# Attention beside two large products: the softmax bias on another engine, value products further behind, and rings of other lengths

## The chip, the cores and the metric

The kernel runs on one core of one Trainium2 chip. The metric is device time in microseconds (us) of one execution. A profiled execution is recorded by the hardware profiler; its span runs from the first instruction to the last. The engines are TensorE (PE; PEld is its weight load), VectorE (DVE), ScalarE (ACT), GpSimd (POOL) and SyncE (SP), which issues nearly all the DMAs. Each engine works through its own queue in order.

## The reference

Two branches are computed from two inputs and set side by side in the output. The first is attention over 2048 positions with 32 heads of 32, where a query sees itself and the 255 keys before it, followed by a product with `wo`. The second is a Fourier mixing layer, as products with given matrices.

```python
qkv = (x @ wqkv).reshape(B, S, 3, H, Dh)           # S 2048, H 32, Dh 32
scores = einsum("bhqd,bhkd->bhqk", q, k) * Dh ** -0.5
mask = (idx[:, None] - idx[None, :] >= 0) & (idx[:, None] - idx[None, :] < 256)
p = softmax(where(mask, scores, -1e9)); o = p @ v
a = o.reshape(B, S, D) @ wo

re = einsum("bsd,ed->bse", xb, dft_hid_re); im = einsum("bsd,ed->bse", xb, dft_hid_im)
b = einsum("ts,bse->bte", dft_seq_re, re) - einsum("ts,bse->bte", dft_seq_im, im)
out = concatenate([a, b], axis=-1)
```

## The kernel before

All products run in 16-bit halves: a value is split into a high half (ACT) and a low half (DVE subtracts the high half from the value), and a product is three passes over the halves. The large products are also taken as seven products of sums and differences of blocks instead of eight, so DVE, POOL and ACT make many sums, splits and evictions beside TensorE.

The program has three parts in time. First come the query, key and value projections. From the middle of these to nearly the end of the Fourier products, attention runs as a side stream between the large products. At the end stands the product with `wo`.

Attention works on 256 blocks. A block is two heads (`hp` picks a pair of the four in a group `g`) times 128 queries (`i`), within a chunk of 512 positions (`sc`). The first 128 blocks take the chunks 0 and 1 of all eight groups, the second 128 the chunks 2 and 3. For one block, `s_step` does this:

- scores on PE (L586) into `s`, and into `old` the oldest 128 keys, which need only a triangle; DVE merges the two (L597) and takes the negative row maxima (`mx`, L602);
- `bias` = maximum times scale plus a shift, on two columns (L609 on POOL; the code holds the same step for ACT at L606, chosen by the constant `BIAS`);
- two exponentials on ACT with that bias (L612), the split into `hl` (ACT L432, DVE L436), a transpose by DMA from SP into `t` (L621), and two mask selects on POOL: `z` from `t` (L627), then `t` in place (L630).

`v_step` takes two blocks: value products on PE into the one bank `pv` (L662), then on DVE a reciprocal, a sum and a multiply into the output `o` (L667 to L673). It stands `LAG` blocks behind the scores. `o_step`, once per group and chunk, splits `o` (ACT L432, DVE L436), transposes it (L684) and stores it (L687). A new group and chunk loads its keys, queries and values with DMAs (`qk1`, `qk0`, `vt`, all through L417); from chunk 2 on the second half of the chunk before is loaded again ahead of the chunk's own keys.

Every buffer belongs to a ring of fixed length. The first instruction that writes buffer k of a ring of n waits for all that use buffer k - n.

What sets the order is a planner inside the program. Every operation is entered with its engine, a cost and what it reads and writes. A due time is worked back from the places of TensorE's work: PE's operations in the order entered, the rest so early that PE is not late. A list scheduler with these costs then picks on each engine the ready operation that is due first. The result is written out as a fixed order for each engine, so a changed constant or ring length changes the order everywhere. `tick` advances attention by one block each time that a set share of the large product's matmuls has been entered.

The large products' own helpers, which the profile names: operands `st` and `reg` from `raw` (ACT L1101, DVE L1102), sums on POOL (L1075), evictions on ACT and DVE (L1193, L1509, L1512).

Of the kernel before, what the change touches and what calls it, by code (L numbers as in the profile page):

```python
# [10 lines left out]
F32 = mybir.dt.float32  # L11
F32R = mybir.dt.float32r
F16 = mybir.dt.float16
# [4 lines left out]
ALU = mybir.AluOpType  # L18
AX = mybir.AxisListType

P = 128
# [3 lines left out]
DH = 32  # L25
HG = 4
# [3 lines left out]
CH = 512  # L30
# [11 lines left out]
DOWN = 2.0 ** -25  # L42
UP = 2.0 ** 25

LAG = 4
LAST = 5
STP = 4
RAWS = 6
TBUF = 6
BIAS = "POOL"  # L50
SUMS = ("POOL", "POOL", "POOL", "POOL")
XSUM = "DVE"
PLAIN = 3
# [280 lines left out]
def fused_kernel(ctx: ExitStack, tc: tile.TileContext, xa, wqk, wv, wo, xb, wd, cs, out):  # L334
# [178 lines left out]
    def att_ring(tag, shape, dtype, n):  # L513
        r = Ring(R, lambda k: pool["att"].tile(shape, dtype, tag=tag, bufs=n, name=f"{tag}_{k}"), n)
        att_rings[tag] = r
        return r

    k_ring = att_ring("qk1", [96, HG, CH], F16, 3)
    q_ring = att_ring("qk0", [96, HG, CH], F16, 2)
    vt_ring = att_ring("vt", [P, QB, HG * VW], F16, 3)  # L520
    mx_ring = att_ring("mx", [P, 2], F32, 6)
    bias_ring = att_ring("bias", [P, 2], F32, 6)
    hl_ring = att_ring("hl", [P, 8 * P], F16, 3)
    t_ring = att_ring("t", [P, 8, P], F16, TBUF)
    z_ring = att_ring("z", [P, 4, P], F16, 4)
    rs_ring = att_ring("rs", [P, 2, 2], F32, 2)
    o_ring = att_ring("o", [P, QB * P], F32, 3)

    def attention():
        blocks = [(g, 2 * pr + sc, hp, i) for pr in range(2) for g in range(NG) for sc in range(2)  # L530
# [103 lines left out]
        def v_step(b):  # L634
            g, sc, hp, i = blocks[b]
            pv = pv_ring.new()
            pvt = lambda: pv.t[:, :4 * VW].rearrange("p (r h w) -> p r h w", r=2, h=2)
            if (g, sc) not in cur:
                cur[g, sc] = o_ring.new()
            for r in (1, 0):  # L640
                qb = sc * QB + i + r
                nb = min(qb + 1, 3)
                nt = min(nb, 2)
                d = st[b + r]
                mats, keys, cost = [], [(d["t"], 0), (d["t"], 1)] + ([d["z"]] if "z" in d else []), 0.0
                seq = [(0, kb) for kb in range(nb)] + [(1, kb) for kb in range(nb)]
                for j in range(2):
                    at = (2 * hp + j) * VW
                    for m, (part, kb) in enumerate(seq):
                        lo = DH * part  # L650
                        k = qb + 1 - nb + kb
                        keys.append(vts[g, k // QB])
                        mats.append((j, lo, part, kb, k, at, m == 0, m == len(seq) - 1, vts[g, k // QB]))
                        cost += 0.0265 if part else 0.0297

                def run(mats=mats, d=d, nb=nb, nt=nt, r=r):
                    for j, lo, part, kb, k, at, a, e, vt in mats:
                        if nb == 3 and kb == 0:
                            lhs = d["z"].t[:, part * 2 + j]
                        else:  # L660
                            lhs = d["t"].t[:, (part * 2 + j) * nt + kb - (nb - nt)]
                        nc.tensor.matmul(pvt()[:, r, j, lo:], lhs, vt.t[:, k % QB, at + lo:at + VW],  # L662
                                         start=a, stop=e, skip_group_check=True)

                op("PE", cost, run, r=list(dict.fromkeys(keys)), w=[pv])
            o, rs = cur[g, sc], rs_ring.new()
            dve(0.173, lambda: nc.vector.reciprocal(rs.t, pvt()[:, :, :, 2 * DH]), r=[pv], w=[rs])  # L667
# [5 lines left out]
            dve(0.29, lambda: nc.vector.tensor_tensor(  # L673
                o.t.rearrange("p (i c) -> p i c", i=QB)[:, i:i + 2, hp * 64:hp * 64 + 64]
                .rearrange("p r (h d) -> p r h d", d=DH), os_(),
                rs.t.unsqueeze(3).to_broadcast([P, 2, 2, DH]), op=ALU.mult), r=[pv, rs], w=[(o, hp, i)])

        def o_step(g, sc):
            o = cur.pop((g, sc))
            keys = [(o, hp, i) for hp in range(2) for i in (0, 2)]  # L680
            ohl, ot = o_ring.new(), o_ring.new()
            half = lambda h: (lambda: ohl.t.bitcast(F16).rearrange("p (h c) -> p h c", h=2)[:, h])
            split(half(0), half(1), lambda: o.t, None, 512, keys, [(ohl, 0)], [(ohl, 1)])
            op("SP", C_TURN, lambda: nc.sync.dma_start_transpose(  # L684
                ot.t.bitcast(F16).rearrange("p (a q) -> p a q", q=P), ohl.t.bitcast(F16)),
               r=[(ohl, 0), (ohl, 1)], w=[ot], dma=turned(8))
            op("SP", C_ISSUE, lambda: nc.sync.dma_start(ots[sc, :, g].rearrange("c h t -> c (h t)"), ot.t.bitcast(F16)),  # L687
               r=[ot], w=[dkey("o", sc, g)], dma=wire(256))

        for b in range(nblk + LAG):  # L690
# [1004 lines left out]
```

## Time and profile before

| | us |
|---|---|
| median of three runs | 1726.13 |
| the three runs | 1724.79, 1728.37, 1726.13 |
| profiled execution, own time | 1728.84 |
| its span | 1727.1 |
| PE busy in the span | 1690.3 |
| DVE, ACT, POOL busy | 1358.8, 1051.5, 771.6 |
| mean granted clock of TensorE | 0.998 of full |

The first scores start at 262 us and the last value products end at 1509 us. Matmuls overlap in the pipeline, so a group's mean duration (379 ns for a matmul of 512 columns) is longer than the distance between two starts. An engine's idle time is named with what ended it, and a wait for several semaphores is put down to the one that came last.

### The profile page before, as it was taken

Reading aid. Unit: us, or ns where it says so; the run is one execution under the profiler, and the core shown is the slowest. Engines: PE = TensorE matmul, PEld = TensorE weight load, DVE = VectorE, ACT = ScalarE, POOL = GpSimd, SP = SyncE. Lnnn points to the kernel's source line nnn. Section 1 sums busy time; section 2 is a strip of 40 time slices with the busy share of each in tenths; the row PEclk is TensorE's granted clock in tenths of the full one; section 3 lists DMA queues with packets and bytes.
Section 4 is the critical chain, followed back from the end, with each engine's and each line's share of the span. In section 5 each row is a group of like instructions: output and inputs, shape, how many; then the busy total and the mean of one; then the engine's idle time right before and its main releaser. Section 6 shows DMA issues by size and latency. Waiting matters only on the chain.

```text
span 1727.1 us, 31901 instructions
## 1 busy us (share of the span) xinstructions
PE 1690.3 (98%) x11607; PEld 908.6 (53%) x11607; DVE 1358.8 (79%) x2294; ACT 1051.5 (61%) x1678; POOL 771.6 (45%) x979
## 2 busy tenths in 40 slices
PE   8999999999999999999999999999999999999998
PEld 3446687675555445555544555545555545544443
DVE  6978997677988888777897986899985679879641
ACT  7555635456757788776675665776665576543322
POOL 0133501224535565635755755676664667611000
PEclk9999999999999999999999999999999999999999
DMA  6388799999998789998599998779999669983331
GB/s 266 121 329 326 229 309 272 267 244 244 221 278 204 159 200 246 215 273 194 98 233 274 246 278 175 151 153 255 238 261 224 141 129 207 215 264 110 110 98 74
DMA packets 469918, 368.36 MB, mean 213 GB/s; under 512 B 341760, under 2 KB 412416, under 8 KB 469760
## 3 DMA queue, kind: packets, MB, share of 16 engines
q1 hardware_dynamic: 468896, 363.17, 81.6%
q0 software_dynamic: 864, 3.15, 1.2%
q8 instruction: 91, 1.49, 0.4%
q14 instruction: 67, 0.55, 0.1%
HBM read 195.97 MB, written 96.86 MB: 170 GB/s over the span
## 4 chain that ended last, share of the span: by engine, by line
PE 83%; DVE 6%; ACT 4%; DMA 3%; issue 3%; POOL 1%; SPq 0%; POOLq 0%; DVEq 0%; ACTq 0%
PE m L720 74%; PE pv L662 4%; PE s L586 3%; PE old L586 1%; DVE st L1102 1%; DMA raw<-in_cs_dram 1%; DVE reg L439 1%; ACT junk L1001 1%; PE m L1323 1%; ACT s L612 1%; ACT reg L432 0%; DVE top L457 0%; DVE mx L602 0%; DVE s L597 0%; DMA late<-in_wo_dram 0%
## 5 line engine op out<-in xcount | busy, mean ns | idle before, releaser
L720 PE MATMUL m<-reg,st 128*128 128x512 f16 x4776 | 1101.1, 379 | 17.5 <-DVE st L1102 3.8
L720 PEld LDWEIGHTS <-st 128*128 128x128 f16 x5400 | 512.4, 98 | 579.1 <-issue 22.0
L612 ACT ACTIVATE s<-s,bias,escs 128x256 f32<-128x256 f32 (+1 forms) x512 | 270.5, 529 | 225.3 <-POOL bias L609 216.3
L609 POOL TENSOR_SCALAR bias<-mx,escs 128x2 f32<-128x2 f32 x256 | 114.2, 446 | 392.2 <-DVE mx L602 334.8
L1075 POOL TENSOR_TENSOR raw<-raw,raw 128x512 f32<-128x512 f32 x128 | 177.4, 1386 | 202.2 <-DVE st L1102 179.8
L436 DVE TENSOR_TENSOR hl<-s,hl 128x512 f16<-128x512 f32 (+1 forms) x256 | 170.6, 668 | 67.6 <-ACT hl L432 64.9
L627 POOL TENSOR_SCALAR_AFFINE_SELECT z<-t 128x512 f16<-128x512 f16 x224 | 174.2, 782 | 53.8 <-DMA t<-hl 41.3
L602 DVE TENSOR_REDUCE mx<-s 128x2 f32<-128x512 f32 (+1 forms) x256 | 170.8, 668 | 4.9
L630 POOL TENSOR_SCALAR_AFFINE_SELECT t<-t 128x512 f16<-128x512 f16 x224 | 169.5, 765 | 9.9
L432 ACT ACTIVATE hl<-s 128x512 f16<-128x512 f32 (+1 forms) x256 | 147.8, 578 | 8.2 <-DMA t<-hl 5.0
L720 PEld LDWEIGHTS <-reg 128*128 128x128 f16 x1212 | 116.3, 98 | 67.2 <-issue 5.2
L1101 ACT ACTIVATE st<-raw,sc 128x1024 f16<-128x1024 f32 x96 | 109.6, 1145 | 59.4 <-PE m L720 30.0
L1102 DVE SCALAR_TENSOR_TENSOR st<-raw,sc,st 128x1024 f16<-128x1024 f32 x96 | 135.8, 1418 | 11.9 <-ACT st L1101 10.7
L586 PEld LDWEIGHTS <-qk 96*128 96x128 f16 x1056 | 93.9, 98 | 81.5 <-issue 8.3
L597 DVE COPY_PREDICATED s<-upper,old 128x256 f32<-128x256 uint32 x224 | 94.6, 422 | 46.6 <-PE old L586 27.2
L720 PE MATMUL m<-reg 128*128 128x512 f16 x480 | 116.3, 382 | 3.5 <-ACT ybig L1509 3.0
L1512 DVE SCALAR_TENSOR_TENSOR ybig<-m,fu,ybig 128x512 f32<-128x512 f32 x112 | 83.4, 745 | 25.4 <-PE m L720 20.9
L720 PE MATMUL m<-xz,st 128*128 128x512 f16 x432 | 97.3, 379 | 2.7 <-ACT m L1193 2.5
L662 PE MATMUL pv<-vt,t 128*128 128x65 f16 x1984 | 98.3, 185 | 0.2
L586 PE MATMUL s<-qk,qk 96*128 96x128 f16 (+1 forms) x608 | 96.1, 253 | 2.0 <-DVE hl L436 1.5
L662 PEld LDWEIGHTS <-t 128*128 128x128 f16 x1984 | 88.3, 96 | 10.8 <-POOL t L630 0.4
L1001 ACT ACTIVATE junk<-raw 128x1024 uint8<-128x1024 f32 x82 | 86.3, 1052 | 10.2 <-DMA raw<-in_cs_dram 9.9
(172 smaller groups left out, 2130.9 us busy)
## 6 DMA issues: line engine op xcount, KB each, us to landing
raw<-in_cs_dram SPq DMA_DIRECT2D x64, 512.0 KB, 5.7
qk<-qs SPq DMA_DIRECT2D x192, 128.0 KB, 3.8
out_dram<-ybig SPq DMA_DIRECT2D x44, 512.0 KB, 4.9
qs<-ybig SPq DMA_DIRECT2D x64, 256.0 KB, 4.5
raw<-in_xb_dram SPq DMA_DIRECT2D x32, 512.0 KB, 5.3
raw<-in_wd_dram SPq DMA_DIRECT2D x32, 512.0 KB, 5.9
ybig<-out_dram SPq DMA_DIRECT2D x32, 512.0 KB, 4.9
vs<-ybig SPq DMA_DIRECT2D x32, 260.0 KB, 4.7
```

The costliest lines, as they stand in the source:

```text
L432: else nc.scalar.activation(dst(), src(), AF.Copy), r=r, w=w)
L436: op("DVE", c_dve(n), lambda: nc.vector.tensor_tensor(dst(), src(), hi(), op=ALU.subtract), r=r, w=w, port=port)
L586: nc.tensor.matmul(dst(j, a, e), qu.t[:, h, i * P:i * P + P], ku.t[:, h, ka:ke], start=True, stop=True, skip_group_check=True)
L602: dve(c_dve(2 * w), lambda: nc.vector.tensor_reduce(mx.t, sv(), axis=AX.X, op=ALU.max, negate=True), r=[(S, 0), (S, 1)], w=[mx])
L609: op("POOL", 0.28, lambda: nc.gpsimd.tensor_scalar(bias.t, mx.t, es, PSHIFT, op0=ALU.mult, op1=ALU.add), r=[mx, ("esc", g // 2)], w=[bias] ...
L612: op("ACT", 0.32 + 0.00085 * w, lambda h=h: nc.scalar.activation(sv()[:, h], sv()[:, h], AF.Exp, bias=bias.t[:, h:h + 1], scale=es), r=[bi ...
L627: op("POOL", 0.637, lambda: nc.gpsimd.affine_select(out=z.t, in_=pk(), compare_op=ALU.is_gt, fill=0.0, base=0, pattern=[[0, 4], [-1, P]], ...
L630: op("POOL", 0.637, lambda: nc.gpsimd.affine_select(out=pk(), in_=pk(), compare_op=ALU.is_ge, fill=0.0, base=0, pattern=[[0, 4], [1, P]], ...
L662: nc.tensor.matmul(pvt()[:, r, j, lo:], lhs, vt.t[:, k % QB, at + lo:at + VW], start=a, stop=e, skip_group_check=True)
L720: nc.tensor.matmul(ps.t[:, j * n:j * n + n], lhs(), rhs(), start=first, stop=last, skip_group_check=True)
L1075: lambda: e.tensor_tensor(o(), a(), b(), op=ALU.subtract if sub else ALU.add), r=r, w=w, port=True)
L1102: op("DVE", c_dve(n, True), lambda: nc.vector.scalar_tensor_tensor(dst(1), src(), scl(), dst(0), op0=ALU.mult, op1=ALU.subtract), r=[*r, s ...
```

## The change

- `BIAS` is "ACT": the bias of a block is an activation on ACT (L606) in place of an instruction on POOL (L609).
- `LAG` 4 becomes 6: value products stand six blocks behind the scores. The rate of `tick` follows from `LAG`, by two blocks in 262.
- `TBUF` 6 becomes 8: eight transposed tiles `t`.
- Keys `qk1` 3 to 2 buffers, values `vt` 3 to 2, masked tiles `z` 4 to 3, outputs `o` 3 to 1.
- `o_step` writes the output's halves into a buffer of the `hl` ring and transposes them into one of the `t` ring, where it took two of the `o` ring. Together they give what the two more `t` tiles take.
- The first value product of a group and chunk reads a key "turn", which the last multiply into the output before it writes.

```diff
-LAG = 4
+LAG = 6
-TBUF = 6
-BIAS = "POOL"
+TBUF = 8
+BIAS = "ACT"
...
-    k_ring = att_ring("qk1", [96, HG, CH], F16, 3)
+    k_ring = att_ring("qk1", [96, HG, CH], F16, 2)
-    vt_ring = att_ring("vt", [P, QB, HG * VW], F16, 3)
+    vt_ring = att_ring("vt", [P, QB, HG * VW], F16, 2)
-    z_ring = att_ring("z", [P, 4, P], F16, 4)
+    z_ring = att_ring("z", [P, 4, P], F16, 3)
-    o_ring = att_ring("o", [P, QB * P], F32, 3)
+    o_ring = att_ring("o", [P, QB * P], F32, 1)
...
-            if (g, sc) not in cur:
+            begins = (g, sc) not in cur
+            if begins:
                 cur[g, sc] = o_ring.new()
...
-                op("PE", cost, run, r=list(dict.fromkeys(keys)), w=[pv])
+                op("PE", cost, run, r=list(dict.fromkeys(keys)) + (["turn"] if begins else []), w=[pv])
...
-                rs.t.unsqueeze(3).to_broadcast([P, 2, 2, DH]), op=ALU.mult), r=[pv, rs], w=[(o, hp, i)])
+                rs.t.unsqueeze(3).to_broadcast([P, 2, 2, DH]), op=ALU.mult), r=[pv, rs], w=[(o, hp, i)] + (["turn"] if hp == 1 and i == 2 else []))
...
-            ohl, ot = o_ring.new(), o_ring.new()
-            half = lambda h: (lambda: ohl.t.bitcast(F16).rearrange("p (h c) -> p h c", h=2)[:, h])
+            ohl, ot = hl_ring.new(), t_ring.new()
+            half = lambda h: (lambda: ohl.t.rearrange("p (h c) -> p h c", h=2)[:, h])
...
```

How the order moves, at three places. A name's first number is its place in its ring's sequence: `s_136` holds the scores of block 136.

On ACT, blocks 136 and 137. Before:

```order
L612 ACTIVATE s_136_11519<-s_136_11519,bias_136_11542,escs_109 128x256 x2
L432 ACTIVATE hl_136_11568<-s_136_11519 128x512
L612 ACTIVATE s_137_11462<-s_137_11462,bias_137_11557,escs_109 128x256 x2
L1101 ACTIVATE st_97_11587<-raw_139_11046,sc_14_11555 128x1024
L1101 ACTIVATE reg1_81<-raw_138_11029,sc_14_11555 128x512
L432 ACTIVATE hl_137_11649<-s_137_11462 128x512
```

Now:

```order
L606 ACTIVATE bias_136_11418<-mx_136_11407,pshift_88,escs_109 128x2
L612 ACTIVATE s_136_11342<-s_136_11342,bias_136_11418,escs_109 128x256 x2
L431 ACTIVATE reg2_82<-raw_149_11316,vwd_103 128x1024
L606 ACTIVATE bias_137_11445<-mx_137_11432,pshift_88,escs_109 128x2
L612 ACTIVATE s_137_11389<-s_137_11389,bias_137_11445,escs_109 128x256 x2
L432 ACTIVATE hl_153_11472<-s_137_11389 128x512
```

The bias stands on ACT just ahead of its exponentials and waits there for DVE's maxima; an operand of the large products stands between the two blocks.

On POOL, sums for the operands and the mask selects around blocks 136 to 140. Before:

```order
L609 TENSOR_SCALAR bias_138_11665<-mx_138_11640,escs_109 128x2
L1075 TENSOR_TENSOR raw_138_11029<-raw_138_11029 128x512
L1075 TENSOR_TENSOR raw_138_11029<-raw_138_11029,raw_139_11046 128x512
L609 TENSOR_SCALAR bias_139_11721<-mx_139_11700,escs_109 128x2
L1075 TENSOR_TENSOR raw_139_11046<-raw_139_11046,raw_138_11029 128x512
L627 AFFINE_SELECT z_104_11740<-t_136_11585 128x512
L609 TENSOR_SCALAR bias_140_11761<-mx_140_11749,escs_109 128x2
L630 AFFINE_SELECT t_136_11585<-t_136_11585 128x4x128
```

Now:

```order
L1076 TENSOR_TENSOR raw_142_11414<-raw_142_11414,raw_141_11448 128x512
L1076 TENSOR_TENSOR raw_141_11448<-raw_141_11448 128x512
L627 AFFINE_SELECT z_108_11918<-t_156_11777 128x512
L627 AFFINE_SELECT z_107_11924<-t_155_11810 128x512
L630 AFFINE_SELECT t_156_11777<-t_156_11777 128x4x128
L630 AFFINE_SELECT t_155_11810<-t_155_11810 128x4x128
```

No bias stands between sums and selects any more.

On SP, around the second load of keys for group 1 of the second half (`qk1_20`), which the scores of block 144 need. Before, `t_138` to `t_141` are the blocks' own transposes:

```order
L621 DMA_TRANSPOSE t_138_11725<-hl_138_11709 128x8x128
L417 DMA qk1_20_11743<-qs_57 32x4x512 x3
L417 DMA raw_144_11755<-in_cs_dram 128x1024
L417 DMA ybig_83<-out_0_dram 128x1024
L417 DMA raw_145_11776<-in_cs_dram 128x1024
L621 DMA_TRANSPOSE t_139_11793<-hl_139_11757 128x8x128
L621 DMA_TRANSPOSE t_140_11825<-hl_140_11790 128x8x128
```

Now, where the output's halves count in the rings too (`t_157` is block 141's, `t_159` block 142's, `t_158` an output's):

```order
L621 DMA_TRANSPOSE t_157_11858<-hl_157_11842 128x8x128
L417 DMA qk1_20_11872<-qs_57 32x4x512 x3
L417 DMA qk0_19_11920<-qs_57 32x4x512
L621 DMA_TRANSPOSE t_159_11933<-hl_159_11905 128x8x128
L685 DMA_TRANSPOSE t_158_11950<-hl_158_11922 128x8x128
L417 DMA qk0_19_11920<-qs_57 32x4x512 x2
```

The load stood ahead of the transposes of blocks 139 to 143; it now stands behind those of 139 to 141, and ahead of two more.

More of the change, by code (lines that the diff above doesn't have):

```diff
@@ L680, in o_step @@
             keys = [(o, hp, i) for hp in range(2) for i in (0, 2)]
-            ohl, ot = o_ring.new(), o_ring.new()
-            half = lambda h: (lambda: ohl.t.bitcast(F16).rearrange("p (h c) -> p h c", h=2)[:, h])
+            ohl, ot = hl_ring.new(), t_ring.new()
+            half = lambda h: (lambda: ohl.t.rearrange("p (h c) -> p h c", h=2)[:, h])
             split(half(0), half(1), lambda: o.t, None, 512, keys, [(ohl, 0)], [(ohl, 1)])
-            op("SP", C_TURN, lambda: nc.sync.dma_start_transpose(
-                ot.t.bitcast(F16).rearrange("p (a q) -> p a q", q=P), ohl.t.bitcast(F16)),
+            op("SP", C_TURN, lambda: nc.sync.dma_start_transpose(ot.t, ohl.t),
                r=[(ohl, 0), (ohl, 1)], w=[ot], dma=turned(8))
-            op("SP", C_ISSUE, lambda: nc.sync.dma_start(ots[sc, :, g].rearrange("c h t -> c (h t)"), ot.t.bitcast(F16)),
+            op("SP", C_ISSUE, lambda: nc.sync.dma_start(ots[sc, :, g].rearrange("c h t -> c (h t)"),
+                                                        ot.t.rearrange("p a q -> p (a q)")),
                r=[ot], w=[dkey("o", sc, g)], dma=wire(256))
```

## The prediction

> **What bounds the kernel now.** I read the page's totals and chain first, then busy time by stage, then who ends TensorE's waits. In the page's first part each engine has busy us, share and instructions; in its chain, shares of the span.
>
> ```profile
> span 1727.1 us, 31901 instructions
> PE 1690.3 (98%) x11607; PEld 908.6 (53%) x11607; DVE 1358.8 (79%) x2294; ACT 1051.5 (61%) x1678; POOL 771.6 (45%) x979
> PE 83%; DVE 6%; ACT 4%; DMA 3%; issue 3%; POOL 1%; SPq 0%; POOLq 0%; DVEq 0%; ACTq 0%
> ```
>
> TensorE sets the end; it is idle for 1727.1 - 1690.3 = 36.8 us. The change adds or removes no matmul, so it can only move this idle time. Where it lies, from a table of stretches (length, then busy us and instructions of PE, PEld, DVE, ACT, POOL; clock; DMA):
>
> ```profile
> 0.00:262.00 262.00, 253.09 (x1529) 152.62 (x1529) 221.80 (x284) 149.07 (x197) 62.46 (x69) 1.00 0.75 263
> 262.00:590.00 328.00, 327.94 (x2510) 193.59 (x2510) 257.86 (x457) 204.31 (x350) 134.81 (x202) 1.00 0.97 239
> 590.00:625.00 35.00, 30.39 (x213) 14.93 (x212) 31.59 (x69) 29.77 (x53) 15.31 (x18) 1.00 0.78 175
> 625.00:860.00 235.00, 234.91 (x1701) 122.44 (x1700) 184.51 (x348) 176.91 (x299) 136.62 (x171) 1.00 0.86 206
> 860.00:960.00 100.00, 94.59 (x649) 47.48 (x648) 87.54 (x158) 66.72 (x106) 59.85 (x68) 1.00 1.03 253
> 960.00:1130.00 170.00, 169.89 (x1320) 90.42 (x1319) 136.05 (x255) 112.05 (x192) 108.48 (x144) 1.00 0.90 205
> 1130.00:1165.00 35.00, 31.32 (x181) 14.96 (x180) 33.26 (x51) 26.62 (x43) 23.47 (x26) 1.00 0.75 165
> 1165.00:1400.00 235.00, 234.63 (x1804) 124.27 (x1802) 186.52 (x358) 146.79 (x244) 145.54 (x193) 1.00 0.94 214
> 1400.00:1425.00 25.00, 21.78 (x104) 10.14 (x103) 17.51 (x30) 17.20 (x30) 13.03 (x13) 0.93 0.77 155
> 1425.00:1510.00 85.00, 85.00 (x667) 44.87 (x665) 74.13 (x146) 49.95 (x83) 59.40 (x72) 1.00 0.96 212
> 1510.00:1575.00 65.00, 59.51 (x267) 26.38 (x266) 53.68 (x64) 30.05 (x33) 12.58 (x8) 0.97 0.67 211
> ```
>
> Attention runs from 262 to 1510. There PE idles 17.5 us, and 16.9 of them in four places: 4.6 at 590, 5.4 at 860, 3.7 at 1130, 3.2 at 1400. They are the passes that make new operands for the transform's second product, where DVE is busy 90%, 88%, 95% and 70%. The 8.9 us before 262 and the 10 us after 1510 lie outside what the change touches. Who ends PE's waits (total us, times, longest), and the two groups of value products, whose last number is PE's idle time before them:
>
> ```profile
> PE m L720 <- ACT m L1193: 5.3, 6, 1.9
> PE m L720 <- DVE st L1102: 3.8, 5, 1.6
> PE m L720 <- DVE ybig L1512: 3.1, 4, 1.4
> PEld L720 <- DVE st L1102: 6.9, 7, 2.1
> L662 PE MATMUL pv<-vt,t 128*128 128x65 f16 x1984 | 98.3, 185 | 0.2
> L662 PE MATMUL pv<-vt,z 128*128 128x65 f16 (+1 forms) x896 | 87.7, 185 | 0.6 <-DVE o L673 0.3
> ```
>
> This reading decides. Value products wait 0.8 us in the whole run, so issuing them later takes no wait off PE by itself. PE waits for operands (st) and evictions (m, ybig) that DVE and ACT reach late, because softmax instructions stand ahead of them in the same queue. The change can help only by letting those softmax instructions stand further back.
>
> **The bias, from POOL to ACT.** POOL's instruction as duration min/median/max ns, its group row, who waited for whom, and the ACT rows that price it:
>
> ```profile
> L609 POOL TENSOR_SCALAR bias<-mx,escs x256: 262/266/1741, 263.7 to 1492.1; 128x2 f32<-128x2 f32 x128
> L609 POOL TENSOR_SCALAR bias<-mx,escs 128x2 f32<-128x2 f32 x256 | 114.2, 446 | 392.2 <-DVE mx L602 334.8 <-DVE rs L667 27.9 <-ACT ybig L431 5.2
> ACT s L612 <- POOL bias L609: 216.3, 130, 4.9
> L612 ACT ACTIVATE s<-s,bias,escs 128x256 f32<-128x256 f32 x480 | 256.8, 536 | 211.5 <-POOL bias L609 203.1
> L612 ACT ACTIVATE s<-s,bias,escs 128x128 f32<-128x128 f32 x32 | 13.7, 429 | 13.7 <-POOL bias L609 13.2
> L1509 ACT ACTIVATE ybig<-m,fu 128x512 f32<-128x512 f32 x32 | 21.7, 680 | 3.3 <-PE m L720 3.3
> L1101 ACT ACTIVATE reg<-raw,sc 128x512 f16<-128x512 f32 x32 | 22.9, 716 | 2.5 <-DVE sc L1066 2.5
> ```
>
> POOL loses 256 x 0.446 = 114.2 us and its 334.8 us of standing at the head of its queue for DVE's maxima, with the mask selects behind. ACT gains 256 instructions of two columns. No such row exists; the exponentials have the same operands: (536 - 429)/128 = 0.84 ns a column, so 429 - 126 x 0.84 = 323 ns at two columns, plus 716 - 680 = 36 for an input in SBUF: 0.36 us, 92 us in all. Bounds: 0.323, and 0.429 (the 128-column row): 83 to 110 us. ACT is busy 830 of the 1248 us of attention (the rows above summed), so 92 lie in its idle time; at 590 it rises from 29.8 to about 32.3 of 35 (seven blocks), near DVE's 31.6. Per block the hop shrinks from 0.446 plus a wait in POOL's queue to 0.36 in front of the exponential. ACT now waits for DVE's maximum where it waited for POOL; behind it stand evictions and operands, as before. On PE directly: 0, since pv waits 0.8.
>
> DVE gains a little too. Its operand split reads 1418 ns beside a busy POOL and 1281 in the first part of the run:
>
> ```profile
> L1102 DVE SCALAR_TENSOR_TENSOR st<-raw,sc,st 128x1024 f16<-128x1024 f32 x96 | 135.8, 1418 | 11.9 <-ACT st L1101 10.7 <-DMA raw<-in_wo_dram 0.9
> L1102 DVE SCALAR_TENSOR_TENSOR st<-raw,scw,st 128x1024 f16<-128x1024 f32 x24 | 30.3, 1281 | 5.2 <-ACT st L1101 4.9 <-issue 0.3
> ```
>
> That is 96 x 0.137 = 13.2 us in which the two hold each other up. The bias is 114.2 of POOL's 771.6 us, 15%, so 2.0 us of DVE come back over the run; I count 0 on PE. The bounds are 0 and 2.0.
>
> The Trainium skill (SBUF — State Buffer, section SBUF: two separate sides) says that VectorE and GpSimd share one pair of ports under an exclusive lock, held for a whole instruction, and that ScalarE waits for nobody. The trace agrees on POOL's side (262 ns at least, 1741 at most). By that rule alone DVE would be free of 32 locks in the four places (6, 17, 6 and 3 biases), 32 x 0.266 = 8.5 us, and an estimate of the gain would be that much at most; the sum here does not use it.
>
> **Six blocks behind, eight transposed tiles.** The spacing of blocks comes from a stretch of the bias rows (length, busy us, count). With it stands the wait of transposes for value products:
>
> ```profile
> 625.00:860.00 235.00, 22.58 (x52) 1.00 0.86 206
> SPq L621 <- PE pv L662: 24.0, 16, 3.0
> ```
>
> A block takes 235/52 = 4.5 us, so two more blocks give each softmax instruction 9 us more until it is due. The planner orders by due times: operands and evictions move ahead of softmax, and SP's queue loses part of the 24.0 us for which transposes stood waiting for a free tile. Is it so in the program's order? When the pair's products are issued on PE, the scores of 4.3 further blocks have been issued on average before, and 6.1 in the changed kernel, in the first half of the 256 blocks. In the second half it is 4.5 and 5.0: there the buffers given up hold the scores back, and most of the slack is not there. The second half begins at about 870 us, and three of the four places lie in it.
>
> So I take 3/4 of the idle time at 590 (3.5 us). At 860 I take half (2.7): there the order spreads the eight blocks from 136 on over 192 product matmuls, where the kernel before crowded them into 104. Of the last two I take a quarter of 6.9 (1.7). The relief is **7.9 us**; its bounds are 0 (DVE's own work fills those places) and 16.9.
>
> **The buffers given up.** Four rings get shorter; what pays is keys, in the second half. With two key buffers the second keys of a group go into the buffer that the last scores of the group before still read. The load is issued only after them; the first scores of the new group wait for it. Loads of queries and keys from 960 us on (min/median/max), and PE's pitch where nothing stalls:
>
> ```profile
> L417 SPq DMA_DIRECT2D qk<-qs x96: 302/432/1831, 967.5 to 1408.9; - x96
> DMA to landing us min/median/max: 1.8/3.7/7.5
> 1600.00:1650.00 50.00, 50.00 (x233) 22.70 (x232) 29.86 (x34) 15.36 (x21) 0.00 (x0) 1.00 0.44 124
> ```
>
> The chain is three issues and a landing: 3 x 0.432 + 3.7 = 5.0 us, at the slowest 1.3 + 7.5 = 8.8. PE's cover is the product matmuls between the two, at 50/233 = 0.2146 us each. In the seven changes of group the order has 60, 60, 24, 32, 52, 28 and 28 of them, where the kernel before had 20, 28, 8, 12, 16, 16 and 28 and needed none. Three have 11 us or more. The thin ones have 5.2, 6.0, 6.0 and 6.9, enough for the median landing, and at the slowest short by 3.6, 2.8, 2.8 and 1.9. Behind the waiting load in SP's queue stand transposes, and value products wait for those. The bounds are 0 and 11.1 us; I take **2.5**, near the lower end since the median fits.
>
> The other three at 0, each with its cover:
>
> ```profile
> POOL z L627 <- PE pv L662: 6.2, 4, 3.1
> L627 POOL TENSOR_SCALAR_AFFINE_SELECT z<-t 128x512 f16<-128x512 f16 x224 | 174.2, 782 | 53.8 <-DMA t<-hl 41.3
> L432 ACT ACTIVATE o<-o 128x512 f16<-128x512 f32 x32 | 20.1, 628 | 9.1 <-DVE o L673 8.3 <-DVE hl L436 0.8
> L436 DVE TENSOR_TENSOR o<-o,o 128x512 f16<-128x512 f32 x32 | 26.3, 822 | 3.0 <-ACT o L432 2.5
> ```
>
> Three masked tiles (z) instead of four: POOL's wait for value products grows from 6.2 us, but a pair needs four selects of about 0.78, 3.1 us of the 9 between products; without that cover products would come 3.1 late per pair. Two value tiles: their reload has the 9 us to the next products, against some 5. One output buffer: its split takes 0.63 + 0.82 = 1.45 us of those 9. The wait of a group's first value product for the output before ("turn") repeats what the single value bank asks for already.
>
> **The sum.** 1728.84 - 7.9 + 2.5 = 1723.4 us for an execution like the profiled one (span 1727.1 and 1.7 around it). The three runs before have their median at 1726.13, 2.7 lower; from it the same -5.4 gives **1720.7 us**.
>
> **The rivals.** First, nothing gained: the four places are full of DVE's own work (95% at 1130), and order cannot help. For it: the slack has mostly gone where three of them lie. Against it: at 1400 DVE is busy only 70%. Relief and price near 2 each: 1726 us. Second, slower: the key reload decides. It wins from the point where the four thin changes of group lose over 2 us each (7.9/4). For it: SP's transposes wait long already, and one blocked load stops the queue. Against it: the median landing fits. With 11.1 us lost and only the 3.5 at 590 regained: 1726.1 + 7.6 = 1733.7 us. Third, all of it: 16.9 back at no price, 1709.2 us. For it: DVE and ACT have idle time on both sides of every place. Against it: 1400 waits for a late load, not for softmax. That the change would not do what it says is half true by the order, and is in the second half's fraction.
>
> **Chances.** Forecast 0.50, no change 0.22, slower 0.18, all 0.10. A measurement of this kernel tells about 0.2% from no change, 3.5 us, so faster means below 1722.7. The forecast's own range, 1713 to 1725, lies mostly below that: 0.43 of its 0.50. With 0.10 from the third rival and 0.02 from the first, faster gets 0.55. Within 0.2%: 0.06 + 0.18, 0.24. Slower: 0.01 + 0.02 + 0.18, 0.21. The range runs from the third rival to the second, 1709 to 1734.
>
> **What would show it.** POOL without the bias row and nearly without waits for DVE's maxima; ACT's bias near 0.36 us, its sum near 92. PE's idle time at 590 should fall from 4.6 to about 1, and at 860 to about 2.7. New waits of PE's scores for a load of keys after 900 us would speak for the second rival, as would transposes that wait longer for scores. The forecast is wrong if the four places keep their idle time, or if ACT becomes the engine that PE waits for at 590.

## The result

| | median us | lowest to highest | executions |
|---|---|---|---|
| kernel before | 1727.25 | 1724.79 to 1729.90 | 6 |
| changed kernel | 1711.39 | 1706.76 to 1713.41 | 6 |

The ratio is 0.9904, with a 95% interval of 0.9888 to 0.9920: 15.9 us less, where 5.4 were forecast. The profiled execution of the changed kernel took 1711.95 us, with a span of 1710.1 (before: 1728.84 and 1727.1).

The totals of the changed kernel, as the prediction showed them of the one before (span, busy us by engine, shares of the chain that ended last):

```profile
span 1710.1 us, 31789 instructions
PE 1686.3 (99%) x11607; PEld 909.7 (53%) x11607; DVE 1346.0 (79%) x2294; ACT 1134.5 (66%) x1934; POOL 668.9 (39%) x723
PE 85%; DVE 6%; ACT 4%; DMA 3%; issue 2%; SPq 0%; DVEq 0%; ACTq 0%
```

The span is 17.0 us shorter. TensorE's idle time is 1710.1 - 1686.3 = 23.8 us in place of 36.8, so 13.0 of the 17.0 are idle time; the other 4.0 are busy time, for the same 11607 matmuls. The same table of stretches as in the prediction (length, then busy us and instructions of PE, PEld, DVE, ACT, POOL; clock; DMA share; GB/s):

```profile
0.00:262.00 262.00, 253.66 (x1531) 153.28 (x1532) 220.78 (x284) 149.48 (x197) 62.37 (x69) 1.00 0.75 262
262.00:590.00 328.00, 325.50 (x2478) 192.06 (x2477) 254.07 (x455) 228.88 (x420) 115.50 (x134) 1.00 0.97 239
590.00:625.00 35.00, 32.81 (x235) 16.84 (x234) 31.32 (x72) 31.73 (x60) 14.16 (x15) 0.95 0.74 168
625.00:860.00 235.00, 233.68 (x1662) 121.29 (x1660) 180.70 (x342) 194.62 (x351) 106.47 (x114) 1.00 0.92 212
860.00:960.00 100.00, 99.56 (x725) 51.74 (x724) 91.14 (x172) 74.58 (x130) 56.61 (x57) 1.00 1.00 251
960.00:1130.00 170.00, 169.04 (x1317) 90.15 (x1316) 136.74 (x255) 126.66 (x231) 100.71 (x109) 1.00 0.90 203
1130.00:1165.00 35.00, 33.95 (x221) 17.24 (x220) 32.78 (x60) 28.12 (x53) 19.06 (x20) 1.00 0.96 215
1165.00:1400.00 235.00, 235.00 (x1783) 124.16 (x1782) 187.97 (x355) 164.76 (x300) 125.04 (x141) 1.00 0.96 213
1400.00:1425.00 25.00, 25.00 (x173) 12.90 (x172) 24.07 (x47) 21.66 (x39) 10.43 (x11) 1.00 0.57 128
1425.00:1510.00 85.00, 84.02 (x605) 42.78 (x604) 67.23 (x129) 46.99 (x78) 48.32 (x52) 1.00 0.96 235
1510.00:1575.00 65.00, 63.86 (x295) 28.53 (x294) 60.55 (x67) 29.56 (x33) 10.20 (x7) 1.00 0.53 180
1575.00:1711.00 136.00, 130.19 (x603) 58.73 (x601) 58.65 (x66) 37.52 (x50) 0.00 (x0) 1.00 0.33 100
```

PE's idle time, length minus busy, against the rows shown before:

| stretch | before | after | difference |
|---|---|---|---|
| to 262 | 8.9 | 8.3 | -0.6 |
| the four places 590, 860, 1130, 1400 | 16.9 | 2.2 + 0.4 + 1.1 + 0.0 = 3.7 | -13.2 |
| the rest of attention, 262 to 1510 | 0.6 | 2.5 + 1.3 + 1.0 + 0.0 + 1.0 = 5.8 | +5.1 |
| 1510 to 1575 | 5.5 | 1.1 | -4.4 |

The later clock times don't hold exactly the same work, since the changed kernel is some 17 us ahead by then. Who ends PE's waits now (total us, times, longest):

```profile
PE m L721 <- ACT m L1194: 7.1, 6, 2.0
PE s L586 <- DVE hl L436: 3.2, 7, 1.0
PEld L721 <- DVE st L1103: 1.7, 4, 1.0
PE pv L663 <- DVE o L674: 1.0, 1, 1.0
PE m L721 <- DVE st L1103: 0.5, 1, 0.5
```

The waits for operands (st), 6.9 and 3.8 us before, are down to 1.7 and 0.5; those for the evictions ybig (3.1 for the half on DVE) are no longer in the list. Nor are those for the half on ACT, which had this row in the kernel before:

```profile
PE m L720 <- ACT ybig L1509: 3.4, 3, 2.7
```

What is left are the evictions that ACT makes, 7.1 us in place of 5.3 + 3.4 = 8.7 (4.6 of the 7.1 between 262 and 1510), and scores that wait until DVE has read the buffer they need (hl). No scores and no weight load waits for a load of keys.

The bias on ACT, and what POOL and DVE make of the room (by line: busy us, mean ns, idle us before and its releasers; the first row has min/median/max ns):

```profile
L606 ACT ACTIVATE bias<-mx,pshift,escs x256: 371/387/402, 263.5 to 1475.3; 128x2 f32<-128x2 f32 x128
L606 ACT ACTIVATE bias<-mx,pshift,escs 128x2 f32<-128x2 f32 x256 | 98.3, 384 | 185.6 <-DVE mx L602 185.1
L627 POOL TENSOR_SCALAR_AFFINE_SELECT z<-t 128x512 f16<-128x512 f16 x224 | 170.0, 766 | 382.2 <-PE pv L663 220.2 <-DMA t<-hl 154.0 <-PE m L721 6.7
L1103 DVE SCALAR_TENSOR_TENSOR st<-raw,sc,st 128x1024 f16<-128x1024 f32 x96 | 130.0, 1357 | 16.0 <-ACT st L1102 15.3
```

ACT takes over the wait for DVE's maxima: 185.1 us where it had waited 216.3 for POOL. POOL, rid of the bias, has time to wait for a free masked tile until value products have read one (220.2 us, 6.2 before). DVE's operand split takes 1357 ns in place of 1418, and DVE's busy time in all fell by 12.8 us, from 1358.8 to 1346.0.

The place at 590 shows the new limit. ACT's own instructions there, one row each (start, duration, what; no row names idle time before it):

```profile
592.49 1.09 ACT L612 ACTIVATE s<-s,bias,escs 128x256 f32<-128x256 f32 x2
593.51 1.04 ACT L432 ACTIVATE reg<-ybig 128x1024 f16<-128x1024 f32 x1
594.46 0.59 ACT L432 ACTIVATE hl<-s 128x512 f16<-128x512 f32 x1
594.94 0.63 ACT L432 ACTIVATE reg<-ybig 128x512 f16<-128x512 f32 x1
595.46 0.59 ACT L1194 ACTIVATE m<-m 128x512 f32<-128x512 f32 x1
595.97 0.62 ACT L432 ACTIVATE reg<-ybig 128x512 f16<-128x512 f32 x1
```

PE's last matmul before the stall starts at 593.78, takes 0.27 and so ends at 594.05; PE's next row, with its idle time and what ended it, is this:

```profile
596.10 1.07 PE L721 MATMUL m<-reg,st 128*128 128x512 f16 x4 [2.05 <-ACT m L1194]
```

PE starts again when the eviction in the fifth row of ACT ends. ACT was never idle: the eviction stood behind a softmax block's exponentials and split and two operands. Before, DVE and ACT each ended part of the 4.6 us lost here; now ACT alone ends what is left, 2.0 of 2.2.

### The profile page after: what moved, and what is told of

Read it like the earlier page. It is cut to its first block, busy times and chain, and to the rows that moved or that the text cites. A ratio compares the mean times of both kernels' runs of the same rounds, so it can differ in the third digit from the quotient of the medians.

```text
span 1710.1 us, 31789 instructions
## 1 busy us (share of the span) xinstructions
PE 1686.3 (99%) x11607; PEld 909.7 (53%) x11607; DVE 1346.0 (79%) x2294; ACT 1134.5 (66%) x1934; POOL 668.9 (39%) x723
## 4 chain that ended last, share of the span: by engine, by line
PE 85%; DVE 6%; ACT 4%; DMA 3%; issue 2%; SPq 0%; DVEq 0%; ACTq 0%
PE m L721 75%; PE pv L663 4%; PE s L586 3%; PE old L586 1%; DMA raw<-in_wd_dram 1%; ACT st L1102 1%; PE m L1324 1%; DMA qk<-qs 1%; DVE reg L439 1%; ACT s L612 1%; DVE top L457 1%; DVE reg L436 1%; DVE hl L436 1%; DVE mx L602 0%; DVE st L1103 0%
## 5 line engine op out<-in xcount | busy, mean ns | idle before, releaser
L627 POOL TENSOR_SCALAR_AFFINE_SELECT z<-t 128x512 f16<-128x512 f16 x224 | 170.0, 766 | 382.2 <-PE pv L663 220.2
L606 ACT ACTIVATE bias<-mx,pshift,escs 128x2 f32<-128x2 f32 x256 | 98.3, 384 | 185.6 <-DVE mx L602 185.1
L630 POOL TENSOR_SCALAR_AFFINE_SELECT t<-t 128x512 f16<-128x512 f16 x224 | 180.6, 814 | 7.6
L1103 DVE SCALAR_TENSOR_TENSOR st<-raw,sc,st 128x1024 f16<-128x1024 f32 x96 | 130.0, 1357 | 16.0 <-ACT st L1102 15.3
```

The source lines that it names most:

```text
L627: op("POOL", 0.637, lambda: nc.gpsimd.affine_select(out=z.t, in_=pk(), compare_op=ALU.is_gt, fill=0.0, base=0, pattern=[[0, 4], [-1, P]], ...
L630: op("POOL", 0.637, lambda: nc.gpsimd.affine_select(out=pk(), in_=pk(), compare_op=ALU.is_ge, fill=0.0, base=0, pattern=[[0, 4], [1, P]], ...
L1103: op("DVE", c_dve(n, True), lambda: nc.vector.scalar_tensor_tensor(dst(1), src(), scl(), dst(0), op0=ALU.mult, op1=ALU.subtract), r=[*r, s ...
```

## Experiments

Three theories stand behind the expectations. **A**: the room counts; with value products further behind, softmax stands further back in the queues of DVE and ACT, and operands and evictions come earlier. **B**: the bias counts; off POOL it shortens the softmax chain and frees POOL's queue and the ports that, as in the prediction, POOL shares with DVE. **D**: the order counts; every edit makes the planner write another order for all engines, some draws are better, and the gain says little of the change. All kernels were timed in five rounds against the kernel before on the same chip (1725.8 to 1727.5 us as median). Idle time in attention is PE's in the one profiled execution of each kernel (it was the fastest in e3, e6, e7 and e10, the slowest in e1, e9, e11 and e12), from 262 us to the last value products, worked out as above.

| | bias on | blocks behind | median us | ratio, 95% | idle in attention, us |
|---|---|---|---|---|---|
| kernel before | POOL | 4 | 1727.25 | 1 | 17.6 |
| e7_cost45 | POOL | 4 | 1730.67 | 1.0021, 1.0012 to 1.0029 | 18.3 |
| e8_turn124 | POOL | 4 | 1718.20 | 0.9943, 0.9931 to 0.9954 | 13.7 |
| e13_before_turn132 | POOL | 4 | 1734.16 | 1.0049, 1.0036 to 1.0062 | 22.2 |
| e1_bias_only | ACT | 4 | 1715.26 | 0.9933, 0.9921 to 0.9944 | 10.6 |
| e3_lag4 | ACT | 4 | 1718.40 | 0.9949, 0.9936 to 0.9962 | 12.6 |
| e2_bias_pool | POOL | 6 | 1715.92 | 0.9934, 0.9922 to 0.9946 | 9.6 |
| changed kernel | ACT | 6 | 1711.39 | 0.9904, 0.9888 to 0.9920 | 9.4 |
| e5_all3 | ACT | 6 | 1714.23 | 0.9930, 0.9914 to 0.9945 | 10.9 |
| e11_after_turn124 | ACT | 6 | 1710.74 | 0.9914, 0.9901 to 0.9927 | 10.4 |
| e12_after_turn132 | ACT | 6 | 1719.33 | 0.9958, 0.9944 to 0.9971 | 12.5 |
| e6_lag8 | ACT | 8 | 1710.10 | 0.9905, 0.9889 to 0.9920 | 7.7 |
| e9_old_order_act | ACT, order made for POOL | 4 | 1739.99 | 1.0065, 1.0048 to 1.0081 | 32.5 |
| e10_new_order_pool | POOL, order made for ACT | 6 | 1739.28 | 1.0070, 1.0058 to 1.0082 | 30.7 |

### One part at a time

The kernel before, with the bias on ACT alone:

```diff
-BIAS = "POOL"
+BIAS = "ACT"
```

> The kernel before with the bias on ScalarE and nothing else. Theory A (the gain comes from value products standing further behind, so that softmax instructions stand further back in the queues of VectorE and ScalarE): 1722 to 1728 us, TensorE idle 32 us or more. Theory B (the gain comes from taking the bias off GpSimd's queue and ports): 1711 to 1717 us, TensorE idle near 24 us as in the changed kernel.

The changed kernel with the bias back on POOL:

```diff
-BIAS = "ACT"
+BIAS = "POOL"
```

> The changed kernel with the bias back on GpSimd. Theory A: 1711 to 1717 us. Theory B: 1722 to 1728 us, with softmax's exponentials waiting some 200 us for the bias again.

The changed kernel, value products four behind:

```diff
-LAG = 6
+LAG = 4
```

> The changed kernel with value products four blocks behind again; eight transposed tiles, the bias on ScalarE and the short rings stay. Theory A: 1720 us or more. Theory B: 1709 to 1715 us.

Measured: the bias alone takes 11.4 us off, the rest without it 10.7 (ratios 0.9933 and 0.9934), both together 15.9. The first is what B had asked for, the second what A had; the changed kernel with four blocks, 1718.40 us, lies between the ranges of both. Neither A nor B alone holds, and the two don't add up. Each leaves its own mark in the waits. PE's waits for operands, in the kernel with the bias alone:

```profile
PEld L720 <- DVE st L1102: 5.2, 7, 1.4
PE m L720 <- DVE st L1102: 1.8, 3, 0.9
PE m L720 <- DVE ybig L1512: 2.8, 3, 1.4
```

in the changed kernel with four blocks:

```profile
PEld L721 <- DVE st L1103: 6.6, 7, 1.6
PE m L721 <- DVE st L1103: 3.2, 4, 1.1
```

and in the changed kernel with the bias on POOL:

```profile
PEld L721 <- DVE st L1103: 3.1, 6, 1.0
PE m L721 <- DVE st L1103: 0.9, 2, 0.5
```

Added up, these two waits for st come to 6.6 to 11.0 us in the six kernels of the table with four blocks behind, whichever engine makes the bias, and to 2.0 to 4.0 in the six with six or eight behind (the last two rows of the table, whose order isn't made for their engine, left out). This is A's mechanism, and it is there in every draw. It goes with the blocks and not with the tiles, since the kernel with four blocks and eight tiles has 9.8 us. The mark of the bias is in the chain of softmax: from the end of the maxima to the start of the exponentials a block takes 1.24 us on average in the kernel before, 1.08 with six blocks and the bias on POOL, and 0.95 and 0.93 in the kernel with the bias alone and in the changed one (worked out from the trace, blocks paired by their order). Over the twelve kernels whose order fits their engine it is 1.08 to 1.31 us with the bias on POOL and 0.91 to 0.97 with it on ACT. How much of TensorE's idle time this shorter chain takes away is not shown.

### The short rings

```diff
-    k_ring = att_ring("qk1", [96, HG, CH], F16, 2)
+    k_ring = att_ring("qk1", [96, HG, CH], F16, 3)
-    vt_ring = att_ring("vt", [P, QB, HG * VW], F16, 2)
+    vt_ring = att_ring("vt", [P, QB, HG * VW], F16, 3)
-    z_ring = att_ring("z", [P, 4, P], F16, 3)
+    z_ring = att_ring("z", [P, 4, P], F16, 4)
```

> The changed kernel with the shortened rings of keys, values and masked tiles at their old lengths (3, 3, 4); one output buffer stays. If the key reload costs 2.5 us as the prediction took it: 1708 to 1709.5 us. If the short rings cost nothing: 1711 us, within 2. If the second rival's lower part holds (more than 5 us): below 1706.

Measured 1714.23 us, with the changed kernel at 1711.39, slightly above all three ranges: the longer rings give nothing back, so the shorter ones cost nothing that can be seen. A price of 2.5 us would be hidden in the spread of orders (below); that the changed kernel pays none is told by its waits, where no load of keys stands. In other draws with two key buffers a price does show: the changed kernel with four blocks has these two rows, 2.7 us together, and the one with the transposes planned at 1.32 has 1.6.

```profile
PEld L586 <- DMA qk<-qs: 1.6, 2, 1.4
PE s L586 <- DMA qk<-qs: 1.1, 1, 1.1
```

### The engine without the order, the order without the engine

The planner's cost stays that of the one engine, and so does the order; the instruction runs on the other. The kernel before with the bias executed on ACT:

```diff
-                op("POOL", 0.28, lambda: nc.gpsimd.tensor_scalar(bias.t, mx.t, es, PSHIFT, op0=ALU.mult, op1=ALU.add),
+                op("POOL", 0.28, lambda: nc.scalar.activation(bias.t, mx.t, AF.Identity, bias=pshift, scale=es),
```

> The order of the kernel before on every engine, with the 256 biases carried out on ScalarE at the places where the planner had set them for GpSimd; the planner still counts them on GpSimd. Theory B (on the chip the bias is late on GpSimd, behind selects, sums and the shared ports): 1713 to 1719 us, as with the bias alone. Theory D (the gain of the bias alone is that of another order): 1724 us or more, since the order is the old one.

The changed kernel with the bias executed on POOL:

```diff
-                op("ACT", 0.387, lambda: nc.scalar.activation(bias.t, mx.t, AF.Identity, bias=pshift, scale=es),
+                op("ACT", 0.387, lambda: nc.gpsimd.tensor_scalar(bias.t, mx.t, es, PSHIFT, op0=ALU.mult, op1=ALU.add),
```

> The order of the changed kernel on every engine, with the biases carried out on GpSimd, at the places where the planner had set them for ScalarE. Theory B: 1722 us or more, since the chain of a block gets a late hop again. Theory D: 1711 to 1716 us.

Measured: 1739.99 and 1739.28 us, both slower than every kernel whose order fits its engines. In the first, an engine that was planned without the bias gets 256 of them; in the second, POOL does. So the first came out as D asked and the second as B did, and the gain that the other theory asked for came in neither. The largest part of the loss is one wait, scores that stand until softmax has emptied their buffer; the kernel before has 1.5 us of it, the changed one 3.2. In the old order with the bias on ACT:

```profile
PE s L586 <- DVE hl L436: 15.9, 16, 7.1
ACT bias L609 <- DVE mx L602: 161.7, 118, 4.5
```

In the new order with the bias on POOL:

```profile
PE s L586 <- DVE hl L436: 11.7, 18, 1.6
ACT s L612 <- POOL bias L606: 288.0, 172, 6.6
```

That is 14.4 of the 14.9 us by which idle time in attention grows in the first, and 8.5 of 21.3 in the second. So the move of the bias by itself, in the order made for POOL, gains nothing and costs 12.5 us; it gains only together with an order that the planner makes for it. These two runs also speak on the shared ports: DVE's busy time falls from 1358.8 to 1356.1 us when the bias leaves POOL in the old order, and from 1346.0 to 1343.8 when it comes back to POOL in the new one. A relief of DVE by some 2 us can't be told from that, and the 12.8 us by which DVE's busy time fell in the changed kernel stay without the bias on ACT. They go with the order; by what in it is not shown.

### Another order for no reason

The kernel before, with the bias planned at a cost near what it takes on POOL (0.446 us):

```diff
-                op("POOL", 0.28, lambda: nc.gpsimd.tensor_scalar(bias.t, mx.t, es, PSHIFT, op0=ALU.mult, op1=ALU.add),
+                op("POOL", 0.45, lambda: nc.gpsimd.tensor_scalar(bias.t, mx.t, es, PSHIFT, op0=ALU.mult, op1=ALU.add),
```

> The kernel before with one number changed: the planner counts the bias on GpSimd at 0.45 us, which the profile measured (446 ns), in place of 0.28. Theory B: 1722 us or more, since the bias stays where it is. Theory D, in the form that the old order trusted a wrong price: 1713 to 1720 us.

The kernel before, with the planned cost of a transpose's issue altered by 0.04 us, which changes nothing but the order:

```diff
-C_TURN = 1.28
+C_TURN = 1.24
```

> The kernel before with a planner's price that concerns nothing in dispute moved slightly: the transposes' issue at 1.24 us, which the profile measured as 1238 ns, in place of 1.28. It tells how far any other order moves the time. Theory B: within 2 us of 1726.7. If the order before was an unlucky one among many: 1714 to 1722 us.

The truer cost gained nothing: 1730.67 us. The neutral one gave 9.2 us, more than half of what the change gave. That speaks for D. So the last runs draw other orders on both sides: the kernel before at 1.32 (e13), and the changed kernel at 1.24, with the edit above (e11), and at 1.32 (e12), with this one:

```diff
-C_TURN = 1.28
+C_TURN = 1.32
```

> The kernel before with the transpose planned at 1.32 us. Theories A/B: the mean of its orders lies above those of the changed kernel by 5 us or more, so about 1718 to 1731 us, as the four orders so far without the change (1717.0 as the mean of those at 1.24, 1727 with none). Theory D: anything from 1709 to 1730, no higher on average than the changed kernel's three.

> The changed kernel, with one planning price altered that has nothing to do with the change: a transpose by DMA is planned at 1.24 us in place of 1.28. What is computed and on which engine stays the same; only the order moves. Theory A/B (the change's own mechanisms give the gain: softmax further back, the bias off GpSimd): every order of this kernel has it, so 1706 to 1716 us. Theory D (the kernel before had an unlucky order, and the changed one a lucky one): orders of both kernels spread over the same stretch; the same repricing took 9.2 us off the kernel before, and this kernel should get worse from its lucky draw, 1714 to 1728 us.

> The same on the other side: the transpose planned at 1.32 us in the changed kernel. Theories A/B: 1706 to 1716 us again. Theory D: 1714 to 1728 us.

(In the first of these three the mean of 1717.0 is a slip: the run at 1.24 had given 1718.2, and the kernel before 1727.) Measured: 1734.16 for the kernel before, above the ranges of both theories, and 1710.74 and 1719.33 for the changed one. D in its full form falls, since the four draws of the kernel before reach from 1718.2 to 1734.2 and the changed kernel's three from 1710.7 to 1719.3, which meet only at the edge; A and B in their full form fall too, since 1719.3 lies outside the 1706 to 1716 they asked for. At equal planning costs the change is worth 0.29% (1.24), 0.96% (1.28) and 0.91% (1.32), on average 0.72% or 12 us. PE's attention stretch at the two ends of the kernel before, first at 1.24, then at 1.32:

```profile
262.00:1504.00 1242.00, 1228.28 (x9139) 663.03 (x9138) 1014.50 (x1864) 831.94 (x1395) 701.58 (x902) 1.00 0.91 219
```

```profile
262.00:1518.00 1256.00, 1233.78 (x9127) 663.05 (x9125) 1012.83 (x1864) 833.52 (x1393) 702.52 (x902) 1.00 0.92 216
```

13.7 and 22.2 us idle: the spread of orders is larger than the relief that was forecast. Why the planner's draws differ by so much was not looked into further.

### Two more blocks again

The changed kernel with eight blocks behind and ten transposed tiles:

```diff
-LAG = 6
-TBUF = 8
+LAG = 8
+TBUF = 10
```

> The changed kernel with value products eight blocks behind and ten transposed tiles, in place of six and eight. Four behind cost 7 us over six (1718.4 against 1711.4). Theory A (room for softmax is what counts): some of the 9.4 us that TensorE still idles in attention comes back, 1706 to 1710 us. Theory D: another draw, 1708 to 1720 us, with no trend.

Measured 1710.10 us (1706.35 to 1711.86), ratio 0.9905: the same as the changed kernel's. Its profiled execution was its fastest, with the least idle time of all:

```profile
262.00:1487.00 1225.00, 1217.34 (x9079) 658.78 (x9077) 998.97 (x1857) 910.11 (x1649) 581.18 (x642) 1.00 0.93 220
```

It lies at the edge of A's range and inside D's, so it doesn't decide between them. Beyond six blocks no further gain can be seen. No run beats the changed kernel by more than its draws differ.

### What follows from all of them

The eight kernels with the bias on ACT, or more room, or both, and an order made for it have ratios of 0.9904 to 0.9958, mean 0.9928. The four with neither have 0.9943 to 1.0049, mean 1.0003. The difference of means is 0.75%, 13 us; with spreads of 0.20% and 0.45% its uncertainty is about 0.24%, an estimate from few draws, four on one side. Idle time in attention doesn't overlap: 7.7 to 12.6 us against 13.7 to 22.2. So most of the gain very likely belongs to the change and would be there, on average, in other draws, and 15.9 is a few us better than that average. Which part gives how much stays open: the three kernels with one part (the one with four blocks keeps the eight tiles and short rings) have a mean of 0.9939, the five with both 0.9922, and these 0.17% are less than draws of one kernel differ. Each part alone brings most of the gain.

Where the idle time goes can be told for one stretch, picked after the fact; clock times hold the same work within some 20 us. From 860 to 1130 us TensorE idles 5.1 to 9.2 us in the six kernels with four blocks behind and 1.4 to 4.4 in the six with more. So there it is the room that counts; the bias alone leaves 5.9 there (first row), and the room alone 3.7 (second):

```profile
860.00:1130.00 270.00, 264.14 (x1956) 136.98 (x1955) 224.99 (x413) 196.70 (x353) 145.55 (x157) 0.99 0.94 220
860.00:1130.00 270.00, 266.29 (x1985) 139.82 (x1985) 225.10 (x415) 180.09 (x295) 175.12 (x215) 1.00 0.93 221
```

From 1130 to 1487 the draws run into each other: the kernel before has 7.3 us, the most of the twelve, its other three draws 3.3 to 6.2, the bias alone 0.5 and the seven others 2.0 to 5.2. From 262 to 860 they do so too, with 3.8 to 6.9 in the four with neither part and 1.2 to 6.4 in the eight others.

## Why the prediction was right, and where not

**What bounds the kernel.** That only TensorE's idle time can move was right for 13.0 of the 17.0 us. The other 4.0 us, fewer busy us for the same matmuls, had no place in the sum; 1.7 of them are clock (last section), the rest is not resolved by a trace whose matmul ends are modelled. It is not peculiar to the two profiles: the four kernels with neither part average 1689.9 us busy (1686.5 to 1693.3), the eight others 1686.7 (1684.0 to 1690.2).

**The deciding reading**, that value products don't wait and that PE waits for operands and evictions behind softmax, held: the waits for st were smaller in every draw with the room.

**The bias.** Estimated at 0.36 us and 92 us in all; it measured 384 ns and 98.3, inside the bounds. By the Trainium skill (ScalarE: Activation LUTs, section What ACT_TABLE_LOAD costs) an activation with immediates takes 186 ns and 0.833 a column, and each per-partition pointer operand adds about 93; with two pointers and two columns an estimate from that page is 374 ns, nearer than the row I went by. ACT at 590 was put at 32.3 of 35 us and measured 31.73. The prediction's own warning, that ACT becomes the engine that PE waits for at 590, came true, and yet the place fell from 4.6 us to 2.2.

**DVE.** The prediction gave DVE 2.0 us back, through the ports, and counted 0 on PE. It got 12.8 us in the changed kernel, but not through the bias leaving POOL: with the bias back on POOL in the same order DVE is busy no longer than without it.

**The relief of 7.9 us.** In attention as a whole PE's idle time fell by 8.1, and by 7.5 from the mean of the four draws with neither part to the mean of the eight others (18.0 to 10.5). The size is right, the places are not: 590 gave 2.4 in place of 3.5, 860 gave 5.0 in place of 2.7, the last two 5.9 in place of 1.7. The four places gave 13.2, and 5.1 came up elsewhere in attention, where now ACT's evictions (2.6), scores behind hl (2.1) and one value product behind the output before it (1.0) hold PE up. By halves it is plainer still: from 262 to 860, where the prediction saw most of the slack, idle time rose from 4.8 to 6.0 us, and from 860 to 1510 it fell from 12.8 to 3.4. So the step that failed is "in the second half ... most of the slack is not there": the places at 860, 1130 and 1400 fell to 1.5 us together. From 860 to 1130 the runs put this down to the room; at 1400 luck had a hand, since from 1380 to 1440 the other three draws of the kernel before idle 0.3 to 1.4 us where it idles 3.4. That the total of 8.1 came so near to 7.9 was luck too. What came up elsewhere had no place in the sum, which had only the key reload as a price.

**The price of 2.5 us for keys** was mis-sized: it measured 0 in the changed kernel, and the ring with three keys brought nothing. In two other draws the wait is there with 2.7 and 1.6 us, so the bound of 11.1 was far, the mechanism not. The prediction let a median load decide and added 2.5 for the slow ones; in the changed kernel none was slow enough to be waited for.

**"The 10 us after 1510 lie outside what the change touches"** was a wrong step. 4.4 us came back between 1510 and 1575. In the kernel before this wait stood there:

```profile
PE m L720 <- DVE reg L1512: 3.3, 2, 2.8
1525.81 6.49 DMA late<-in_wo_dram
```

DVE's eviction stood behind a split whose input was a late load (the second row, from the chain that ended last), and this order is written by the same planner. The wait is absent in the changed kernel, and present with 2.4 us in the changed kernel with the bias on POOL and with 1.8 in the one with the transposes planned at 1.24. The kernel before has the most idle time after attention of all draws, so part of this gain is its bad luck.

**At 0**, SP's transposes, masked tiles and the single output buffer: the transposes' wait for value products fell from 24.0 us to 7.6, the masked tiles' rose to 220.2 on POOL and reached PE nowhere. Value products waited once for the multiply into the output, 1.0 us; the kernel with the bias alone, which has three output buffers, has 2.3 us of this wait, so it is not shown to come from the single buffer.

**The rivals.** No change fell, and so did the slower one, by the missing waits for keys. The third, all 16.9 us back at no price (1709.2), comes nearest in time, but not by its mechanism: the four places kept 3.7, 5.1 arose elsewhere, and tail and busy time made it up. What was missing is a rival that isn't about the change at all: that a new order by itself moves the time by 10 us either way. With it the range would have stood on a measured ground; a neutral edit of the kernel before gave -9.2 and +8.3.

So the forecast of 5.4 was too small mainly by three terms: the price that wasn't there (2.5), the tail (4.4) and busy time (4.0). With 0.2 of relief and 0.6 before 262 they make 11.7, up to rounding the 11.6 between it and the 17.0 of the two spans.

## What to carry to other kernels

Where a planner writes the order, price an edit against the spread of neutral orders: alter one planning cost by a few per cent in both kernels, and compare draws with draws before believing a gain below that spread. An instruction moved to another engine in an unchanged order can cost more than the move saves; plan it where it runs. Don't add up two remedies for stalls behind the same queues: here 11.4 and 10.7 us made 15.9 together. And when a place is cleared, look for idle time that comes up elsewhere: here it was 5.1 us against 13.2.

## What the hardware showed

TensorE's granted clock falls to half after idle time of some 2 us, in a kernel where it is busy 98%. Four stretches of the kernel before, each 3.41 us long; the column behind the engines is the granted clock:

```profile
1413.96:1417.37 3.41, 2.35 (x14) 1.08 (x12) 1.38 (x7) 1.21 (x3) 0.00 (x0) 1.00 1.23 235
1417.37:1420.78 3.41, 1.25 (x6) 0.58 (x6) 1.07 (x3) 3.38 (x7) 0.27 (x1) 1.00 0.15 58
1420.78:1424.19 3.41, 3.41 (x10) 1.37 (x9) 2.15 (x4) 3.38 (x7) 1.26 (x1) 0.50 0.69 147
1424.19:1427.60 3.41, 3.41 (x19) 1.67 (x18) 3.41 (x8) 1.69 (x5) 2.58 (x4) 1.00 0.22 84
```

PE is busy 1.25 us in the second stretch, and the whole third runs at half clock: 10 matmuls start where 19 do in the fourth. The changed kernel does it once, behind the stall at 590:

```profile
593.54:596.95 3.41, 1.36 (x7) 0.62 (x6) 3.25 (x6) 3.41 (x7) 0.00 (x0) 1.00 0.32 124
596.95:600.36 3.41, 3.41 (x10) 1.32 (x9) 3.34 (x12) 2.51 (x6) 0.00 (x0) 0.50 0.33 94
```

The Trainium skill (TensorE: Matmul & The Clock Gate, section What's actually happening) has free-running windows of 3413 ns, and a clock that is halved after an idle one. The traces agree on the windows: where a profile has several such stretches, their starts lie a whole number of 3.413 us apart (1420.78 and 1536.83 in the kernel before: 34.0). They differ on what counts as idle. Eleven of the fourteen profiles have half clock before the program's end. Each of the 17 times that it set in, the window before held 1.66 to 2.61 us of idle time, and no window with more than 1.91 went without; between 1.66 and 1.91 both occur. A window of 1.91 us that no half clock follows, in the new order with the bias on POOL:

```profile
600.82:604.23 3.41, 1.50 (x9) 0.75 (x8) 3.41 (x7) 3.41 (x7) 0.00 (x0) 1.00 0.39 137
604.23:607.64 3.41, 3.41 (x19) 1.65 (x18) 3.34 (x12) 3.35 (x7) 0.64 (x1) 1.00 0.41 112
```

About half a window idle is enough, in one stall or in several short ones (in the kernel before with the bias planned at 0.45, stalls of 0.60, 0.60 and 0.47 us were enough). By the starts, 10 against 19, each time costs about half of 3.41 us beside the stall itself, an estimate: 3.4 us in the kernel before and 1.7 in the changed one, so 1.7 of the 17.0.
